# An order of work that knows of PSUM banks, and transposes that leave the score buffers

## The chip, the cores and the metric

The kernel runs on one core of a Trainium2 chip. The metric is the device time of one execution in microseconds. Before the change the median of three runs is 1225.1 us (1224.89 to 1226.91).

The core's engines work side by side, each through its own queue in order: TensorE (PE) multiplies matrices and transposes, and writes only to PSUM; VectorE (DVE), ScalarE (ACT) and GpSimd (POOL) work element by element; SyncE (SP) issues the transfers. PSUM has banks of 512 fp32 columns. The kernel's eight banks are: score buffers `s0` and `s1` (two banks each), `o` (two banks, the sums of the feed-forward block's output), `h` (one bank, its hidden layer, in halves `h0` and `h1`) and `pv` (one bank).

## The reference

Attention over 8 batches, 8 heads, 576 positions and head size 64, with a threshold below the row's maximum, and then a feed-forward block with a squared ReLU:

```
scores = scale * (q @ k.T)
thresh = max(scores, axis=-1) - tau
scores = where(scores >= thresh, scores, -1e9)
attn   = exp(scores - max) / (sum + 1e-9)
x      = (attn @ v), heads joined          # 4608 tokens x 512
h      = x @ w_in                          # 512 -> 2048
g      = s * relu(h)**2 + b
out    = g @ w_out                         # 2048 -> 512
```

All of it is fp32.

## The kernel before

**Visits and tiles.** A visit is a pair of heads and half of the queries of a batch: 64 visits, `Visit` objects numbered `n`. A tile is 128 queries against 576 keys. A visit of the first half has four tiles; one of the second half has a fifth, with the last 64 queries of both heads. For each tile PE writes scores into a score buffer (L373 for pairs of tiles, L362 for the fifth tile, L384 and L395 in later visits); DVE scales them and takes the minimum of the negated row (L416), ACT takes the exponential (L427), DVE applies the threshold and sums (L430), DVE takes the reciprocal (L433). From visit 4 on POOL scales the weights by it (L435); in visits 0 to 3 this is done after the values.

**Turning the weights.** The value product needs the weights with keys on the partitions. In visits 0 to 7 (`vs.pe`, `PE_VISITS = 8`) PE transposes them: four blocks of 128 columns into `tp` (L447) and the last 64 columns into `tt` (L445); ACT copies both into `er` (L456 and L454). Before the change `tt` is the first 128 columns of the tile's own score buffer, whose scores begin at column 224, so both share a bank. `tp` is `h` for even tiles of visits 0 to 3, and `pv` otherwise. From visit 8 on DVE transposes, and PE takes no part.

**Score buffers.** `scores_in` (L295) gives a tile its buffer: in visits 0 to 3 the three of `s0`, `s1` and `o` in turn; in visits 4 to 11 (`late`) `s0` and `s1` for the two tiles of a pair; later `s0` and `s1` in turn.

**Values and feed-forward block.** The value products of a visit (L498, L507) go through `pv`, from where ACT and DVE take x (L520 to L528). When four visits have given the x of 256 tokens, a block follows: 16 steps, each with a product into a half of `h` (L637), ReLU, square and rounding on ACT (L644 to L647), a remainder on POOL (L648) and two products into `o` (L654). The weights of the block are unpacked once, during the first block, by ACT, DVE and POOL (L582 to L596).

**The order of the work.** No engine's order is written by hand. Each step of each engine is put into a plan (`Plan.add`) with a cost, the keys that it reads and writes, and a due time. `Plan.ordered` builds an order forward or backward by list scheduling, `Plan.played` plays it with random delays, and `Plan.run` takes the best of 27 settings with 8 rounds each, by the mean over `SLOW` (a seed, and a factor on PE's costs early on). Keys are names such as `"s0"`; `(sk, "t")` is the key of the transposed 64 columns. In this plan they are no part of `"s0"`. When the kernel is built, accesses of two engines to one bank of a buffer are nevertheless put one after the other, in the order that the plan gave, by waits on semaphores.

Of the kernel before, what the change touches and what calls it, by code (L numbers as in the profile page):

```python
# [32 lines left out]
class Plan:  # L33
# [6 lines left out]
    SLOW = (1, 1.2), (2, 1.3), (3, 1.5), (4, 1.3)  # L40
# [6 lines left out]
    def add(self, engine, cost, emit, r=(), w=(), at=0.0, port=False, tiled=False):  # L47
# [12 lines left out]
        self.ops.append((engine, cost[0], cost[-1], emit, deps, at, port or engine == "POOL", tiled))  # L60
# [32 lines left out]
    def played(self, order, seed, cold, hand=60, to_pe=150, same=40):  # L93
        ops, free, done, port, mode = self.ops, {}, [0.0] * len(self.ops), 0.0, False
        late = random.Random(seed)
        for _, n in order:
            e, busy, ready, _, deps, _, shared, tiled = ops[n]
# [21 lines left out]
            done[n] = t + busy + tail  # L119
        return max(done) / 1000  # L120

    def ordered(self, before, after, rank, busy, done, back):
# [10 lines left out]
        order, port, mode = [], 0.0, False  # L133
        for _ in ops:
# [17 lines left out]
            if e == "PE" and mode and not ops[n][7]:  # L152
                for at, m in sorted(there[e]):
                    if ops[m][7] and at < rank[n] + self.NEAR:
# [8 lines left out]
            if ops[n][6] and port > t + self.PASS:  # L163
                for at, m in sorted(there[e]):
                    if not ops[m][6] and busy[m] < port - t + self.OVER:
                        there[e].remove((at, m))
                        heapq.heapify(there[e])
                        heapq.heappush(there[e], (rank[n], n))
                        n = m
                        break  # L170
            if ops[n][6]:
                t = max(t, port)
                port = t + busy[n]
            order.append((t, n))
# [17 lines left out]
def tile_attention_ffn(ctx: ExitStack, tc: tile.TileContext, qT, kT, v, tau, w_in, w_out, s, b, out):  # L192
# [91 lines left out]
    class Visit:  # L284
# [10 lines left out]
        def scores_in(self, i, j):  # L295
            return f"s{i % 2}" if self.split else f"s{j}" if self.late else ("s0", "s1", "o")[i % 3]
# [59 lines left out]
    def scores(vs, i, t):  # L356
        n = vs.n
        if t is None:
# [4 lines left out]
            pe(970, both, [("k", n)] + vs.kd, ["s0"], i - SCORES_AHEAD)  # L363
# [13 lines left out]
    def split_scores(vs, i, j, t):  # L377
# [8 lines left out]
        pe(531, products, [(x, j) for x in ("z", "qh", "ql")], [sk], i - SCORES_AHEAD)  # L386
# [22 lines left out]
    def tile_of(vs, i, j, t):  # L409
# [28 lines left out]
        if vs.pe:  # L438
            tt, kt = ps[0:T, 0:P], (sk, "t")
            kp = ["pv"] if vs.late or i % 2 else ["h0", "h1"]  # L440
            tp = bank[kp[0].strip("01")]
            tp = tp.rearrange("p (c q) -> p c q", c=NQ)

            def transposes():
                nc.tensor.transpose(out=tt, in_=ev[:, M:S], identity=ident)  # L445
# [4 lines left out]
            for h, n0, c0, c1 in parts:  # L450
                nn = (c1 - c0) // 32
                e = er[:, vs.n, h, n0:n0 + nn].rearrange("p n (c q) -> p c n q", c=5)
                ke = [("er", vs.n, h, n0 + n) for n in range(nn)]
                act((46 + 28 * nn, 146 + 28 * nn), lambda e=e, c0=c0, c1=c1, nn=nn: nc.scalar.copy(  # L454
                    out=e[0:T, NQ], in_=tt[:, c0:c1].rearrange("p (n q) -> p n q", n=nn)), [kt], ke, i + 0.5)
                act((68 + 100 * nn, 176 + 100 * nn), lambda e=e, c0=c0, c1=c1, nn=nn: nc.scalar.copy(  # L456
                    out=e[:, 0:NQ], in_=tp[:, :, c0:c1].rearrange("p c (n q) -> p c n q", n=nn)), kp + ke, ke, i + 0.5)
# [152 lines left out]
    class Block:  # L610
# [16 lines left out]
        def step(self, f, at):  # L627
# [10 lines left out]
            if f in (0, NF - 1):  # L638
                for c in range(0, NC, 2):
                    pe(6 * 120.9, lambda c=c: products(range(c, c + 2)), [("xh", c // 2), ("xl", c // 2), (f"w{f}", "i")], ["h0", "h1"], at)  # L640
            else:
                pe(3 * NC * 120.9, lambda: products(range(NC)), [(x, c) for x in ("xh", "xl") for c in range(2)] + [(f"w{f}", "i")],
# [222 lines left out]
```

## Time and profile before

| | |
|---|---|
| median of three runs | 1225.1 us |
| the profiled execution's own time | 1225.36 us |
| its span | 1223.5 us |
| PE busy | 1194.7 us (98%) |
| DVE busy | 802.5 us (66%) |
| ACT busy | 766.9 us (63%) |
| POOL busy | 700.8 us (57%) |
| chain that ended last, PE's share | 94% |

The span runs from the first to the last instruction of one profiled execution. Busy time is the time in which an engine has at least one instruction under way; a wait is idle time of an engine, put down to the instruction whose end released it. The chain that ended last goes back from the last instruction to what released it, step by step.

### The profile page before, as it was taken

How to read it: one execution, taken by the hardware profiler on the slowest of the kernel's cores; microseconds unless marked ns; L12 is line 12 of the kernel's file. 1: busy time of each engine (PE TensorE's matmuls, PEld its weight loads, DVE VectorE, ACT ScalarE, POOL GpSimd, SP SyncE). 2: the span in 40 equal slices, each digit the busy share in tenths (PEclk: the TensorE clock that was granted, in tenths of full speed). 3: DMA queues.
4: the chain of work that ended last, by engine and by line, in shares of the span. 5: the costliest groups of instructions: out<-in, count | busy, mean ns of one | idle time of the engine just before them, and what ended most of it. 6: DMA issues, size and time to landing. Idle time of an engine off the chain costs nothing.

```text
span 1223.5 us, 24575 instructions
## 1 busy us (share of the span) xinstructions
PE 1194.7 (98%) x7958; PEld 987.4 (81%) x7958; DVE 802.5 (66%) x2162; ACT 766.9 (63%) x1890; POOL 700.8 (57%) x806
## 2 busy tenths in 40 slices
PE   7789999999999999999999999999999999999998
PEld 5467778888887888878887888888888888878987
DVE  7997876777776776756666667666666576663021
ACT  5777756666665765666666666566656665654443
POOL 1466845766665775656675666667656675652200
PEclk8999999999999999999999999999999999999999
DMA  8661256677767766666566756556756666652000
GB/s 301 210 206 43 64 137 157 155 184 184 179 153 173 185 169 162 155 157 169 138 172 166 172 142 157 142 151 159 193 137 158 156 159 152 170 134 69 4 18 18
DMA packets 259536, 180.69 MB, mean 148 GB/s; under 512 B 83536, under 2 KB 238160, under 8 KB 259408
## 3 DMA queue, kind: packets, MB, share of 16 engines
q1 hardware_dynamic: 259120, 178.98, 57.5%
q8 instruction: 64, 1.05, 0.4%
q14 instruction: 64, 0.52, 0.1%
q10 hardware_dynamic: 288, 0.13, 0.0%
HBM read 87.03 MB, written 9.44 MB: 79 GB/s over the span
## 4 chain that ended last, share of the span: by engine, by line
PE 94%; DVE 3%; ACT 1%; issue 1%; DMA 0%; ACTq 0%; DVEq 0%
PE h L637 34%; PE o L654 33%; PE pv L507 13%; PE s L384 9%; PE s L373 2%; PE s L395 1%; DVE s L416 1%; DVE k L587 1%; PE pv L447 1%; DVE tr L430 0%; DMA qr<-in_q_dram 0%; DVE em L430 0%; PE s L445 0%; ACT em L427 0%; ACT er L456 0%
## 5 line engine op out<-in xcount | busy, mean ns | idle before, releaser
L637 PE MATMUL h<-xh,w 128*128 128x256 f32 x2304 | 467.0, 284 | 1.2 <-ACT g L644 1.2
L637 PEld LDWEIGHTS h<-xh,w 128*128 128x128 f32 x2304 | 377.5, 190 | 28.1 <-issue 7.6
L654 PE MATMUL o<-w,gh 128*128 128x512 f32 x1152 | 364.9, 398 | 0.6 <-DVE em L674 0.6
L416 DVE TENSOR_SCALAR_CACHE_REDUCE s<-s,nsc 128x576 f32<-128x576 f32 x283 | 230.4, 820 | 153.8 <-PE s L384 119.5
L648 POOL TENSOR_TENSOR gl<-g,gh 128x256 fp32r<-128x256 f32 x272 | 204.6, 753 | 212.7 <-ACT gh L647 187.1
L637 PE MATMUL h<-xl,w 128*128 128x256 f32 x1152 | 325.1, 282 | 0.0
L435 POOL TENSOR_SCALAR em<-em,st,zero 128x576 f32<-128x576 f32 x262 | 220.0, 841 | 139.2 <-DVE st L433 94.1
L430 DVE SCALAR_TENSOR_TENSOR em<-s,st,em 128x577 f32<-128x577 f32 x268 | 217.0, 811 | 83.9 <-ACT st L425 54.1
L427 ACT ACTIVATE em<-s,st 128x576 f32<-128x576 f32 x268 | 197.7, 738 | 66.9 <-DVE s L416 41.0
L654 PEld LDWEIGHTS o<-w,gh 128*128 128x128 f32 x1152 | 196.5, 189 | 35.1 <-issue 11.3
L654 PE MATMUL o<-w,gl 128*128 128x512 f32 x576 | 224.5, 390 | 0.0
L644 ACT ACTIVATE g<-h 128x256 f32<-128x256 f32 x288 | 110.4, 383 | 181.2 <-PE h L637 165.4
L637 PEld LDWEIGHTS h<-xl,w 128*128 128x128 f32 x1152 | 219.0, 190 | 5.5
L468 DVE STREAM_TRANSPOSE tr<-em 128x512 f32<-128x512 f32 x252 | 178.1, 707 | 52.0 <-POOL em L435 45.4
L507 PE MATMUL pv<-er,vb 128*64 128x256 f32 (+1 forms) x1280 | 170.3, 411 | 0.0
L349 POOL TENSOR_TENSOR k<-kr,k 64x576 fp32r<-64x576 f32 x104 | 149.0, 1434 | 37.1 <-ACT k L348 26.9
L647 ACT CAST gh<-g 128x256 fp32r<-128x256 f32 x288 | 116.2, 404 | 43.2 <-PE o L654 40.2
L384 PE MATMUL s<-k 128*128 128x288 f32 x832 | 142.4, 296 | 0.0
L507 PEld LDWEIGHTS pv<-er,vb 128*64 128x64 f32 x1280 | 85.7, 136 | 66.8 <-issue 11.8
L384 PEld LDWEIGHTS s<-k 128*128 128x128 f32 x832 | 127.2, 188 | 15.3 <-issue 2.4
L654 PEld LDWEIGHTS o<-w,gl 128*128 128x128 f32 x576 | 108.2, 188 | 24.6
L645 ACT ACTIVATE g<-g 128x256 f32<-128x256 f32 x288 | 120.0, 417 | 4.8
(108 smaller groups left out, 939.5 us busy)
## 6 DMA issues: line engine op xcount, KB each, us to landing
er<-tr SPq DMA_DIRECT2D x448, 160.0 KB, 3.2
kr<-in_k_dram SPq DMA_DIRECT2D x116, 288.0 KB, 4.1
vb<-in_v_dram SPq DMA_DIRECT2D x128, 128.0 KB, 3.0
qr<-in_q_dram SPq DMA_DIRECT2D x56, 160.0 KB, 4.3
er<-tr SPq DMA_DIRECT2D x112, 80.0 KB, 2.3
w<-in_moe_w_in_dram SPq DMA_DIRECT2D x16, 512.0 KB, 6.3
w<-in_moe_w_out_dram SPq DMA_DIRECT2D x16, 512.0 KB, 5.4
out_dram<-oo SPq DMA_DIRECT2D x30, 256.0 KB, 2.3
```

The costliest lines, as they stand in the source:

```text
L349: pool((1500, 1500), lambda: nc.gpsimd.tensor_tensor(out=z()[D:P], in0=kr[D:P, j], in1=z()[D:P].bitcast(F32), op=ALU.subtract), rk + [("z" ...
L384: nc.tensor.matmul(flat[sk][:, S0 + hf * HS:S0 + (hf + 1) * HS], lazy["q"][:, x, j, qc], lazy["k"][:, j, cs], start=(x == 0), stop=(x == 1))
L416: dve((740, 875), lambda: nc.vector.tensor_scalar(out=ps[:, S0:S0 + S], in0=ps[:, S0:S0 + S], scalar1=nsc, scalar2=None, op0=ALU.mult, op1 ...
L427: act((632, 740), lambda: nc.scalar.activation(out=ev, in_=ps[:, S0:S0 + S], func=AF.Exp, bias=st8[:, 0:1], scale=-1.0), [sk, (ks_, 0)], [ ...
L430: dve((742, 830), lambda: nc.vector.scalar_tensor_tensor(out=eb, in0=ps[:, S0:S0 + S + 1], scalar=st8[:, 1:2], in1=eb, op0=ALU.is_le, op1= ...
L435: pool((795, 825), lambda: nc.gpsimd.tensor_scalar(out=ev, in0=ev, scalar1=st8[:, 4:5], scalar2=zero, op0=ALU.mult, op1=ALU.add), [em_k, ( ...
L468: nc.vector.transpose(out=to[:, :, 0:NQ].rearrange("p m c q -> p m (c q)"), in_=ev[:, 0:M].rearrange("p (m r) -> p m r", m=4))
L507: nc.tensor.matmul(ps[j * D:(j + 1) * D, 0:32 * nb], vb[r, n, j, c], er[r, n, j, 0:nb, 32 * c:32 * c + 32], start=(c == 0), stop=(c == 4))
L637: nc.tensor.matmul(ps, w[:, c, :], x[:, c, :], start=(c == 0 and i == 0), stop=(c == NC - 1 and i == 2))
L645: act((322, 417), lambda: nc.scalar.activation(out=g, in_=g, func=AF.Square), [f"g{k}"], [f"g{k}"], at)
L648: do((712, 740), lambda: eng.tensor_tensor(out=lo, in0=g, in1=hi.bitcast(F32), op=ALU.subtract), [f"g{k}", f"gh{n}"], [f"gl{n}"], at)
L654: nc.tensor.matmul(bank["o"][:, t, :], a[:, ts_], w, start=(f == 0 and i == 0), stop=(f == NF - 1 and i == 2))
```

## The change

It has three parts.

1. The plan notes for each step which PSUM banks it touches and whether it writes there (`banks`, `use`). `free_at` lets a step start only when the last accesses of other engines to the bank are over, where one of the two writes; `used` notes the access. `played` and `ordered` both apply it. If a step would have to wait for a bank or for the port that DVE and POOL share by more than `PASS`, another ready step of the engine may go first.
2. In visits 0 to 3 scores use `s0` and `s1` alone. The transposes become two steps: even tiles use `h` for the 512 columns and `o[:, 1]` for the 64, odd tiles `o[:, 0]` and `pv`. In visits 4 to 7 both go through `pv`: 512 columns, their copies, then the 64 columns into the same bank, and their copies.
3. Constants of the plan change: the factors of `SLOW`, and some costs of PE's steps. The second products name `o0` or `o1` in place of `o`. A guard column for scores in `o` is no longer set.

```diff
-    SLOW = (1, 1.2), (2, 1.3), (3, 1.5), (4, 1.3)
+    SLOW = (1, 1.0), (2, 1.1), (3, 1.3), (4, 1.1)
...
+        use = {b: False for k in r for b in self.banks(k)}
+        use.update((b, True) for k in (*w, *(r if engine == "PE" else ())) for b in self.banks(k))
+        self.ops.append((engine, cost[0], cost[-1], emit, deps, at, port or engine == "POOL", tiled, tuple(use.items())))
+
+    def banks(self, k):
+        k, t = k if isinstance(k, tuple) and len(k) == 2 else (k, None)
+        if k == "o":
+            return [f"o{t}"] if t in (0, 1) else ["o0", "o1"]
+        return [k] if k in ("s0", "s1", "pv", "o0", "o1") else ["h"] if k in ("h0", "h1") else []
+
+    def free_at(self, n, t, last, tail, hand):
+        for b, writes in self.ops[n][8]:
+            for e, wrote, at, rest in last.get(b, ()):
+                if e != self.ops[n][0] and (writes or wrote):
+                    t = max(t, at + (rest if tail is None else tail) + hand)
+        return t
+
+    def used(self, n, at, rest, last):
+        for b, writes in self.ops[n][8]:
+            was = last.get(b, []) if not writes else []
+            last[b] = [u for u in was if u[1] or u[0] != self.ops[n][0]] + [(self.ops[n][0], writes, at, rest)]
...
+            if ops[n][8]:
+                t = self.free_at(n, t, last, None, to_pe if e == "PE" else hand)
...
+        def delay(n, t):
+            at = max(t, port) if ops[n][6] else t
+            if not ops[n][8]:
+                return at - t
+            hand = self.TO_PE if ops[n][0] == "PE" else self.HANDOVER
+            return self.free_at(n, at, last, done[n] - busy[n] if back else None, hand) - t
...
+            wait = delay(n, t)
+            if wait > self.PASS:
+                for at, m in sorted(there[e]):
+                    if delay(m, t) <= self.PASS and busy[m] < wait + self.OVER:
+                        there[e].remove((at, m))
+                        heapq.heapify(there[e])
+                        heapq.heappush(there[e], (rank[n], n))
+                        n, wait = m, delay(m, t)
+                        break
+            t += wait
...
-            return f"s{i % 2}" if self.split else f"s{j}" if self.late else ("s0", "s1", "o")[i % 3]
+            return f"s{i % 2}" if self.split else f"s{j}"
...
-            pe(970, both, [("k", n)] + vs.kd, ["s0"], i - SCORES_AHEAD)
+            pe(760, both, [("k", n)] + vs.kd, ["s0"], i - SCORES_AHEAD)
...
-            tt, kt = ps[0:T, 0:P], (sk, "t")
-            kp = ["pv"] if vs.late or i % 2 else ["h0", "h1"]
-            tp = bank[kp[0].strip("01")]
+            if vs.late:
+                tp, kp = bank["pv"], ["pv"]
+                tt, kt = tp[0:T, 0:P], kp
+            elif i % 2:
+                tt, kt, tp, kp = bank["pv"][0:T, 0:P], ["pv"], bank["o"][:, 0], ["o0"]
+            else:
+                tt, kt, tp, kp = bank["o"][0:T, 1, 0:P], ["o1"], bank["h"], ["h0", "h1"]
...
-            pe(575, transposes, [em_k, "ident"], [kt] + kp, i + 0.5)
...
+            pe(390, whole, [em_k, "ident"], kp, i + 0.5)
+            if kt != kp:
+                pe(90, rest, [em_k, "ident"], kt, i + 0.5)
+            copies(True)
+            if kt == kp:
+                pe(90, rest, [em_k, "ident"], kt, i + 0.5)
+            copies(False)
...
-                pe(3 * 231.3, lambda t=t: second(t), [f"gh{n}", f"gl{n}", (f"w{f}", "o")],
-                   [("o", t)] + (["o"] if f == 0 else []), at + SECOND)
+                pe(3 * 230.4, lambda t=t: second(t), [f"gh{n}", f"gl{n}", (f"w{f}", "o")],
+                   [("o", t)] + ([f"o{t}"] if f == 0 else []), at + SECOND)
```

`whole` holds the four transposes of 128 columns, `rest` the one of 64; `copies(True)` makes the copies of the first, `copies(False)` those of the second.

## Rows read from the trace of the kernel before

**Rows 1.** The page: busy time of an engine, busy tenths and clock in 40 slices.
```profile
PE 1194.7 (98%) x7958; PEld 987.4 (81%) x7958; DVE 802.5 (66%) x2162; ACT 766.9 (63%) x1890; POOL 700.8 (57%) x806
...
PE   7789999999999999999999999999999999999998
...
PEclk8999999999999999999999999999999999999999
```

**Rows 2.** Busy time by stage: stretch, its length, busy us of each engine, clock.
```profile
9.00:80.00 71.00, 53.52 (x338) 34.97 (x338) 67.54 (x187) 53.22 (x112) 27.19 (x22) 0.89 0.78 262
80.00:112.00 32.00, 32.00 (x212) 23.95 (x209) 27.12 (x70) 25.69 (x65) 25.72 (x23) 1.00 0.27 84
112.00:122.00 10.00, 7.96 (x53) 5.97 (x51) 6.69 (x18) 6.11 (x16) 3.56 (x5) 1.00 0.01 2
...
200.00:1100.00 900.00, 900.00 (x6096) 753.79 (x6095) 619.98 (x1687) 579.39 (x1446) 576.37 (x663) 1.00 0.66 161
1100.00:1223.50 123.50, 117.64 (x738) 102.72 (x736) 21.78 (x49) 50.67 (x127) 19.13 (x26) 1.00 0.10 27
```

**Rows 3.** Waits of PE and of DVE, 9 to 80 us: total, times, longest.
```profile
PE s L373 <- DVE tr L430: 2.9, 2, 2.4
PE pv L447 <- ACT er L456: 2.4, 3, 1.2
PE pv L447 <- DVE x L521: 1.9, 2, 1.6
PE s L445 <- ACT tr L427: 1.8, 2, 1.5
...
PE s L373 <- ACT er L454: 1.4, 1, 1.4
...
DVE s L416 <- PE s L373: 3.0, 2, 2.7
...
DVE s L416 <- PE s L445: 0.9, 1, 0.9
DVE s L416 <- ACT er L454: 0.7, 2, 0.4
```

**Rows 4.** PE's instructions in order of time, 53 to 78 us: start, length, instruction, idle before.
```profile
53.16 1.24 PE L373 MATMUL s<-kr,qr 64*128 64x288 f32 x8 [0.50 <-DVE tr L430]
...
60.66 1.97 PE L373 MATMUL s<-kr,qr 64*128 64x288 f32 x8
...
68.13 0.66 PE L447 MATMUL pv<-k,em 128*128 128x128 f32 x4 [0.38 <-DVE x L521]
...
70.43 0.66 PE L447 MATMUL pv<-k,em 128*128 128x128 f32 x4 [1.21 <-ACT er L456]
70.84 0.36 PE L637 MATMUL h<-xh,w 128*128 128x256 f32 x1
...
77.26 0.27 PE L445 MATMUL s<-k,tr 128*64 128x128 f32 x1 [1.49 <-ACT tr L427]
```

**Rows 5.** ACT's instructions in order of time, 69 to 116 us.
```profile
69.64 0.26 ACT L454 COPY er<-s 64x128 f32<-64x128 f32 x1 [0.91 <-DVE s L416]
...
76.37 0.74 ACT L427 ACTIVATE tr<-s,st 128x576 f32<-128x576 f32 x1
...
114.72 0.26 ACT L454 COPY er<-s 64x128 f32<-64x128 f32 x1 [3.16 <-PE s L373]
114.88 0.58 ACT L456 COPY er<-pv 128x512 f32<-128x512 f32 x1
```

**Rows 6.** PE's instructions in order of time, 115 to 121 us.
```profile
115.51 0.66 PE L447 MATMUL pv<-k,em 128*128 128x128 f32 x4 [0.59 <-ACT er L456]
...
117.04 0.38 PE L637 MATMUL h<-xh,w 128*128 128x256 f32 x1 [0.17 <-ACT g L644]
...
120.01 0.27 PE L445 MATMUL s<-k,tr 128*64 128x128 f32 x1 [1.27 <-DVE tr L430]
```

**Rows 7.** DVE's instructions in order of time, 115 us.
```profile
115.01 0.83 DVE L416 TENSOR_SCALAR_CACHE_REDUCE s<-s,nsc 128x576 f32<-128x576 f32 x1 [2.13 <-ACT er L454]
```

**Rows 8.** DVE's L587: its group from 9 to 80 us; its durations, whole span.
```profile
L587 DVE SCALAR_TENSOR_TENSOR k<-w,k 128x512 int32<-128x512 int32 x14 | 12.0, 857 | 0.0
...
L587 DVE SCALAR_TENSOR_TENSOR k<-w,k x28: 669/685/1635, 21.8 to 142.9; 128x512 int32<-128x512 int32 x28
```

More of the change, by code (lines that the diff above doesn't have):

```diff
@@ L94, in played @@
         ops, free, done, port, mode = self.ops, {}, [0.0] * len(self.ops), 0.0, False
-        late = random.Random(seed)
+        late, last = random.Random(seed), {}
         for _, n in order:
-            e, busy, ready, _, deps, _, shared, tiled = ops[n]
+            e, busy, ready, _, deps, _, shared, tiled, _ = ops[n]
             t = free.get(e, 0.0)
@@ L119, in played @@
             done[n] = t + busy + tail
+            if ops[n][8]:
+                self.used(n, t + busy, tail, last)
         return max(done) / 1000
@@ L132, in ordered @@
                 heapq.heappush(coming[o[0]], (0.0, n))
-        order, port, mode = [], 0.0, False
+        order, port, mode, last = [], 0.0, False, {}
+        def delay(n, t):
[4 more added lines that the diff above has]
+            return self.free_at(n, at, last, done[n] - busy[n] if back else None, hand) - t
         for _ in ops:
@@ L162, in ordered @@
                 mode = ops[n][7]
[L163 to L170, printed above, removed]
             if ops[n][6]:
-                t = max(t, port)
                 port = t + busy[n]
+            if ops[n][8]:
+                self.used(n, t + busy[n], done[n] - busy[n], last)
             order.append((t, n))
@@ L385, in products @@
                                      start=(x == 0), stop=(x == 1))
-        pe(531, products, [(x, j) for x in ("z", "qh", "ql")], [sk], i - SCORES_AHEAD)
+        pe(526, products, [(x, j) for x in ("z", "qh", "ql")], [sk], i - SCORES_AHEAD)
     def last_rows(vs, i, before):
@@ L442, in tile_of, with whole, rest @@
             tp = tp.rearrange("p (c q) -> p c q", c=NQ)
-            def transposes():
-                nc.tensor.transpose(out=tt, in_=ev[:, M:S], identity=ident)
+            def whole():
                 for c in range(NQ):
                     nc.tensor.transpose(out=tp[:, c], in_=ev[:, c * P:(c + 1) * P], identity=ident)
-            pe(575, transposes, [em_k, "ident"], [kt] + kp, i + 0.5)
+            def rest():
+                nc.tensor.transpose(out=tt, in_=ev[:, M:S], identity=ident)
@@ L449, in tile_of, with copies @@
             parts = [(j, 4 * t, 0, P)] if t is not None else [(h, NB // 32, h * T, h * T + T) for h in range(2)]
[L450 to L457, printed above, removed]
+            def copies(first):
+                for h, n0, c0, c1 in parts:
+                    nn = (c1 - c0) // 32
+                    e = er[:, vs.n, h, n0:n0 + nn].rearrange("p n (c q) -> p c n q", c=5)
+                    ke = [("er", vs.n, h, n0 + n) for n in range(nn)]
+                    if first:
+                        act((68 + 100 * nn, 176 + 100 * nn), lambda e=e, c0=c0, c1=c1, nn=nn: nc.scalar.copy(
+                            out=e[:, 0:NQ], in_=tp[:, :, c0:c1].rearrange("p c (n q) -> p c n q", n=nn)), kp, ke, i + 0.5)
+                    else:
+                        act((46 + 28 * nn, 146 + 28 * nn), lambda e=e, c0=c0, c1=c1, nn=nn: nc.scalar.copy(
+                            out=e[0:T, NQ], in_=tt[:, c0:c1].rearrange("p (n q) -> p n q", n=nn)), kt + ke, ke, i + 0.5)
@@ L639, in step @@
                 for c in range(0, NC, 2):
-                    pe(6 * 120.9, lambda c=c: products(range(c, c + 2)), [("xh", c // 2), ("xl", c // 2), (f"w{f}", "i")], ["h0", "h1"], at)
+                    pe(6 * 120, lambda c=c: products(range(c, c + 2)), [("xh", c // 2), ("xl", c // 2), (f"w{f}", "i")], ["h0", "h1"], at)
             else:
-                pe(3 * NC * 120.9, lambda: products(range(NC)), [(x, c) for x in ("xh", "xl") for c in range(2)] + [(f"w{f}", "i")],
+                pe(3 * NC * 120, lambda: products(range(NC)), [(x, c) for x in ("xh", "xl") for c in range(2)] + [(f"w{f}", "i")],
                    ["h0", "h1"], at)
@@ L726, in guards @@
     def guards():
-        for n in "s0", "s1", "o":
+        for n in "s0", "s1":
             nc.vector.memset(flat[n][:, S0 + S:S0 + S + 1], -3e38)
```

3 lines of the change are left out of this document (1 added, 2 removed).

## Prediction

> **What bounds the kernel now.** I read the page first, then busy time by stage, then who waits for whom in the stages where TensorE is not full, and last the few microseconds around each such wait. On the page TensorE (PE) is busy 98% of the span, and the slices below nine tenths are the first three and the last; its granted clock is below nine tenths in the first slice alone [rows 1]. The stages say the same in microseconds [rows 2]: from 200 to 1100 us PE is busy 900.00 of 900.00 us at clock 1.00, so no order of the work can gain anything there except by giving PE less to do, and the change takes no matmul away. What is left is 9 to 80 us, where PE idles 71.00 - 53.52 = 17.5 us, the stretch from 112 to 122 us, where it idles 10.00 - 7.96 = 2.0 us, and the end (123.50 - 117.64 = 5.9 us), which holds no transposes and which the change leaves alone. Between 9 and 80 us the engine to look at is VectorE (DVE): busy 67.54 of 71.00 us, 95%. PE's matmuls for the feed-forward block begin at 70.84 us [rows 4]; until then PE lives on what DVE hands it. So a gain has to come from idle DVE before about 70 us or from idle PE behind it, some 20 us altogether, and most of those are waits for real data.
>
> **What the trace shows of the banks.** In the kernel before, the last 64 columns of a tile are transposed into the first 128 columns of a score buffer (L445) and copied out by ScalarE (ACT) at L454. Those columns share a bank with the scores. In visits 4 to 7 a tile's weights are scaled by POOL (L435) before PE may transpose them, so a wait of L445 on ACT's exponential (L427) can't be one for its data: it is the exponential of another tile that is reading the same bank. The trace has such waits in every direction: PE's L445 for L427, 1.8 us; PE's scores for the copy L454, 1.4 us; DVE's L416 for L445 and for L454, 0.9 and 0.7 us [rows 3]. From 112 to 122 us they form one chain: L454 starts at 114.72 after ACT idled 3.16 us behind scores that PE writes in that bank [rows 5], DVE's L416 starts at 115.01 after 2.13 us behind L454 [rows 7], and PE, which has run out of other work, waits 0.59 us for pv, 0.17 us for g and 1.27 us for the threshold (L430) [rows 6].
>
> **The change part by part.**
> *The 64 columns leave the score buffers (all eight visits).* Terms that go:
> - the hole from 112 to 122 us, 0.59 + 0.17 + 1.27 = 2.0 us [rows 6]. PE is the bound around it, so it counts in full.
> - the wait of 1.49 us of L445 at 77.26 us for an exponential that starts at 76.37 us [rows 4, 5]. Feed-forward matmuls stand behind it in PE's queue; counted in full, 1.5 us.
> - the wait of 1.21 us of pv at 70.43 us [rows 4]: ACT's L454 before it had idled 0.91 us for DVE's L416 in the same bank [rows 5]; 0.9 us.
> - DVE's waits for L445 and L454 from 9 to 80 us, 0.9 + 0.7 = 1.6 us [rows 3]. DVE is the bound there, so PE's waits of the same stretch don't count again; but a DVE that is early helps PE only where PE then has work, so I take the middle between 0 and 1.6, 0.8 us. The ends are 0 and, with PE's 1.4 us, 3.0 us.
> Sum: 2.0 + 1.5 + 0.9 + 0.8 = 5.2 us.
>
> *In visits 4 to 7 both transposes go through pv, one after the other.* PE transposes 512 columns, ACT copies (0.58 us), and only then PE transposes the other 64 (0.27 us) and ACT copies again (0.26 us); a handover is 0.05 us (the copy that starts at 114.88 ends at 115.46, PE starts at 115.51) [rows 5, 6]. pv is held 0.27 + 0.05 + 0.26 + 0.05 = 0.63 us longer per tile, for 20 tiles. Behind the second transpose wait, in PE's queue, whatever the plan put there, and everything else that needs pv: the next tile's transposes and the value products. After 80 us feed-forward matmuls can stand between (PE is busy 32.00 of 32.00 us from 80 to 112 us [rows 2]) and the cost is nothing; if that cover failed, each tile would pay 0.63 us. Ahead of 80 us there is hardly any cover. Bounds: 0 and 20 x 0.63 = 12.6 us. I take the places in these visits where PE already waits for pv before 80 us: at 68.13 us (0.38 us, for x to be read out by L521) and at 70.43 us [rows 4]; 2 x 0.63 = 1.3 us.
>
> The row just used shows PE waiting 1.21 us for a bank that ACT is still emptying. The Trainium skill ("Perfetto Trace Analysis", section "Matmuls") says that independent matmul groups should rotate through different PSUM banks, so that emptying one overlaps filling the next. By that rule the second pass through pv costs at every tile, 12.6 us by the upper bound, not at two; the trace agrees before 80 us, and after it shows the wait covered.
>
> *Visits 0 to 3 use two score buffers in place of three; "o" and "h" or pv and "o" take the transposes.* The scores of a pair of tiles can then be written only when both tiles before are through L430. PE needs 1.24 us for a pair at full clock and 1.97 us at the lower one [rows 4], and DVE has no tile work meanwhile. Its other work (unpacking weights) fills such gaps: L587 alone is 12.0 us from 9 to 80 us [rows 8]. Bounds: 0, and 7 pairs x 1.97 = 13.8 us. I take 0: visits 4 to 7 already run on two buffers, and DVE's busy share of 95% covers part of them as well [rows 2].
>
> *The plan's model and constants.* It moves every instruction, the DMAs on SP among them; no wait that PE or DVE has from 9 to 80 us is for SP or POOL among the larger ones [rows 3]. What it can still win is DVE's stretching: L587 takes 857 ns in the mean of 14 against a median of 685 ns, 14 x 0.172 = 2.4 us [rows 8], while POOL works beside it. Ends: 2.4 us won, and as much lost; I take 0. One memset fewer and five transposes per tile as before: 0.
>
> Sum: 5.2 - 1.3 = 3.9 us off. The profiled execution took 1225.36 us (1.86 us outside its span), so 1221.5 us. The median of the runs, 1225.1 us, lies 0.3 us lower; the forecast is 3.6 us or 0.29% below it. A difference under 0.2% (2.45 us) is what I call no change.
>
> **The rivals.**
> *pv takes the place of the score buffers.* Four tiles of visits 4 to 7 pass through pv before 80 us (the last at the row of 77.26 us), and about as many where PE runs out of other work as it does from 112 to 122 us. If seven pay 0.63 us in place of two, 3.2 us more go: 1221.5 + 3.2 = 1224.7 us, no change. For it: PE's waits on pv are already 2.4 and 1.9 us from 9 to 80 us [rows 3]. Against it: a plan that knows the bank can put value products or scores between the two passes. The rule of the Trainium skill ("Perfetto Trace Analysis", section "Matmuls") leads here too.
> *Two score buffers starve DVE.* In visits 0 to 3 the gap of a pair that no weight work covers costs between 1.24 and 1.97 us, 1.6 in the middle. Five uncovered gaps of seven cost 8.0 us: 1221.5 + 8.0 = 1229.5 us, slower. It decides from four gaps on (3.6 us of gain plus 2.45 us, over 1.6 us). For it: DVE waits 3.0 us for scores already, PE 2.9 us for DVE to be through with a buffer [rows 3]. Against it: 2.7 us of those 3.0 are the first wait, before any scores exist, and there is more weight work than gaps.
> *The feed-forward work starts earlier too.* Nothing is lost at pv and DVE's stretching goes: 5.2 + 2.4 = 7.6 us, 1217.8 us. For it: the plan now sees every wait that it schedules around. Against it: the stretching is no matter of banks.
> *The change doesn't do what it says:* the new order keeps as many waits, in other places, 1225 us.
>
> **How the numbers follow.** Forecast 0.38, pv 0.27, starved DVE 0.17, earlier start 0.13, no effect 0.05. About a fifth of the forecast's case lies within 0.2% of the median, and a little of pv's lies on either side: faster 0.30 + 0.13 + 0.02 = 0.45, the same 0.08 + 0.21 + 0.04 = 0.33, slower 0.17 + 0.04 + 0.01 = 0.22. The range reaches from 1215.5 us (the earlier start with the 3.0 us of the upper end in place of 0.8) to 1228.5 us (short of five starved gaps). The forecast's own range is 1218.5 to 1223.5 us.
>
> **What would show it.** Right: no wait of L416 for the copy of the 64 columns and none of the transposes for L427; from 112 to 122 us (or where visits 4 to 7 end) PE full; PE's idle time from 9 to 80 us smaller by 2 to 4 us; the page's PE busy time the same within 2 us. pv as rival: waits of the transposes for the copies (L456 before) over 5 us in total. Starved DVE: waits of L416 for scores (L373) beyond 3.0 us, and DVE under 93% busy from 9 to 80 us. I am wrong in kind if the idle time after 200 us changes, since no step above reaches there.

## The result, and the profile after

The changed kernel takes 1232.92 us (median of 5 runs, 1232.47 to 1234.28) against 1225.87 us for the kernel before, measured beside it: a ratio of 1.0054, 95% interval 1.0043 to 1.0066. I forecast 1221.5 us. The change made the kernel slower, and the time lies outside the range.

The page of the kernel after, the lines that answer to [rows 1], with its chain that ended last:

```profile
PE 1193.8 (97%) x7958; PEld 985.8 (80%) x7958; DVE 802.6 (65%) x2161; ACT 766.8 (62%) x1890; POOL 702.0 (57%) x806
...
PE   6789999999999999999999999999999999999998
...
PEclk7899999999999999999999999999999999999999
...
PE 92%; DVE 4%; DMA 2%; ACT 1%; issue 1%; SPq 0%; POOL 0%; DVEq 0%; ACTq 0%
```

PE has as many instructions as before, x7958, and is busy 0.9 us less, in a span that is 7.2 us longer (1230.7 against 1223.5 us). So all of the loss is PE standing idle, 8.1 us more of it. The stages of the kernel after (stretch, length, busy us of PE, PEld, DVE, ACT and POOL, clock) say where; after them stand three of the kernel before, for stretches that [rows 2] does not have as rows of their own:

```profile
9.00:80.00 71.00, 50.29 (x323) 32.38 (x324) 66.58 (x181) 51.69 (x106) 29.24 (x22) 0.86 0.77 258
112.00:122.00 10.00, 9.31 (x57) 7.10 (x56) 8.57 (x19) 7.78 (x18) 6.66 (x6) 1.00 0.06 22
122.00:150.00 28.00, 26.65 (x175) 19.93 (x175) 21.05 (x50) 21.67 (x59) 20.21 (x23) 1.00 0.13 34
...
80.00:200.00 120.00, 115.65 (x753) 87.69 (x752) 93.55 (x238) 84.84 (x208) 73.25 (x81) 1.00 0.37 97
200.00:1100.00 900.00, 896.97 (x6061) 752.05 (x6060) 614.12 (x1673) 574.79 (x1439) 574.58 (x659) 1.00 0.66 160
1100.00:1230.70 130.70, 125.91 (x803) 109.44 (x801) 26.92 (x63) 54.15 (x138) 22.94 (x31) 1.00 0.13 34
```

```profile
0.00:9.00 9.00, 5.53 (x26) 4.77 (x26) 1.13 (x9) 1.28 (x1) 1.98 (x15) 0.92 0.71 219
...
122.00:150.00 28.00, 28.00 (x188) 20.94 (x188) 23.07 (x52) 21.68 (x57) 22.16 (x25) 1.00 0.18 47
...
80.00:200.00 120.00, 117.96 (x769) 91.11 (x766) 92.11 (x232) 82.38 (x208) 76.13 (x82) 1.00 0.37 96
```

PE's idle time grows from 17.5 to 20.7 us between 9 and 80 us [rows 2], from 2.0 to 4.4 us between 80 and 200 us, and from nothing to 3.0 us between 200 and 1100 us; before 9 us it grows by 0.6 us (9.00 - 4.96 against 9.00 - 5.53), and after 1100 us it shrinks by 1.1 us. The hole from 112 to 122 us shrinks, as forecast, to 0.7 us idle in place of 2.0 us. But the 1.3 us are not won: from 122 to 150 us, where PE had no idle time before, it now idles 1.4 us, and all 2.0 us of idle time from 112 to 150 us are waits for copies out of pv. The waits (who waited for whom: total us, times, longest) name what came instead, for PE over the whole span and, in the last line, for DVE from 9 to 80 us:

```profile
PE h L484 <- DVE tr L464: 6.7, 3, 3.8
PE pv L548 <- ACT er L499: 6.3, 3, 2.7
PE h L484 <- DVE em L464: 5.0, 2, 2.8
PE pv L487 <- ACT er L496: 2.7, 4, 0.9
...
PE pv L484 <- ACT er L499: 1.5, 3, 0.6
PE o L704 <- DVE oo L724: 1.4, 3, 0.8
...
PE pv L557 <- ACT er L499: 0.5, 1, 0.5
...
DVE s L450 <- PE s L407: 5.7, 6, 2.3
```

And of the kernel before, PE's waits that answer to the first three lines:

```profile
PE o L445 <- DVE tr L430: 1.6, 1, 1.6
PE s L445 <- DVE tr L430: 1.4, 2, 1.3
...
PE pv L498 <- ACT er L456: 1.3, 1, 1.3
```

In the kernel after, L407 writes scores, L450 scales them, L464 is the threshold, L484 and L487 are the transposes of the 512 and of the 64 columns, L496 and L499 their copies, L548 the first value product. No transpose waits for another tile's exponential any more, and L450 waits for no copy: every wait inside the score buffers that [rows 3], [rows 6] and [rows 7] show is gone. In their place PE waits 11.7 us for thresholds before it can transpose (6.7 + 5.0, against 1.6 + 1.4 before) and 6.3 us for the copies before a value product (against 1.3), and DVE waits 5.7 us for scores against 3.0 us.

PE's instructions in order of time show the pattern (start, length, instruction, idle before):

```profile
42.07 0.27 PE L487 MATMUL pv<-k,em 128*64 128x128 f32 x1
46.11 1.12 PE L484 MATMUL h<-k,tr 128*128 128x128 f32 x4 [3.77 <-DVE tr L464]
...
47.37 2.10 PE L407 MATMUL s<-kr,qr 64*128 64x288 f32 x8
...
52.38 0.99 PE L484 MATMUL h<-k,em 128*128 128x128 f32 x4 [2.22 <-DVE em L464]
...
64.65 0.66 PE L548 MATMUL pv<-k,st 128*64 128x128 f32 x8 [2.73 <-ACT er L499]
...
70.24 0.30 PE L487 MATMUL pv<-k,em 128*64 128x128 f32 x1 [0.86 <-ACT er L496]
71.11 0.63 PE L484 MATMUL pv<-k,em 128*128 128x128 f32 x4 [0.58 <-ACT er L499]
...
72.60 0.49 PE L687 MATMUL h<-xh,w 128*128 128x256 f32 x1
```

With two score buffers a pair of tiles goes through as one, and PE and DVE run in lockstep: PE writes both, DVE and ACT work on both, and PE has nothing to write meanwhile, because both buffers are taken (3.77 and 2.22 us). Then PE runs and DVE waits for scores. The feed-forward matmuls begin at 72.60 us, 1.8 us later than in [rows 4].

### The profile page after: what moved, and what is told of

Read it like the earlier page. It is cut to its first block, busy times and chain, and to the rows that moved or that the text cites. A ratio compares the mean times of both kernels' runs of the same rounds, so it can differ in the third digit from the quotient of the medians.

```text
span 1230.7 us, 24541 instructions
## 1 busy us (share of the span) xinstructions
PE 1193.8 (97%) x7958; PEld 985.8 (80%) x7958; DVE 802.6 (65%) x2161; ACT 766.8 (62%) x1890; POOL 702.0 (57%) x806
## 4 chain that ended last, share of the span: by engine, by line
PE 92%; DVE 4%; DMA 2%; ACT 1%; issue 1%; SPq 0%; POOL 0%; DVEq 0%; ACTq 0%
PE h L687 33%; PE o L704 32%; PE pv L557 13%; PE s L418 9%; PE s L407 2%; PE s L429 1%; DVE s L450 1%; DMA qr<-in_q_dram 1%; PE pv L484 1%; DVE em L464 0%; ACT em L461 0%; DVE tr L464 0%; DVE xl L673 0%; DVE k L637 0%; DMA vb<-in_v_dram 0%
## 5 line engine op out<-in xcount | busy, mean ns | idle before, releaser
L450 DVE TENSOR_SCALAR_CACHE_REDUCE s<-s,nsc 128x576 f32<-128x576 f32 x288 | 234.1, 821 | 157.8 <-PE s L418 119.9
L464 DVE SCALAR_TENSOR_TENSOR em<-s,st,em 128x577 f32<-128x577 f32 x270 | 218.5, 812 | 98.3 <-ACT st L459 58.9
L557 PE MATMUL pv<-er,vb 128*64 128x256 f32 (+1 forms) x1280 | 171.9, 414 | 1.5 <-DMA out_dram<-oo 1.0
L557 PEld LDWEIGHTS pv<-er,vb 128*64 128x64 f32 x1280 | 86.5, 137 | 67.9 <-issue 11.6
```

The source lines that it names most:

```text
L450: dve((740, 875), lambda: nc.vector.tensor_scalar(out=ps[:, S0:S0 + S], in0=ps[:, S0:S0 + S], scalar1=nsc, scalar2=None, op0=ALU.mult, op1 ...
L464: dve((742, 830), lambda: nc.vector.scalar_tensor_tensor(out=eb, in0=ps[:, S0:S0 + S + 1], scalar=st8[:, 1:2], in1=eb, op0=ALU.is_le, op1= ...
L557: nc.tensor.matmul(ps[j * D:(j + 1) * D, 0:32 * nb], vb[r, n, j, c], er[r, n, j, 0:nb, 32 * c:32 * c + 32], start=(c == 0), stop=(c == 4))
```

## The experiments

I held three theories. **Theory 1:** the new buffers cost by themselves (1a two score buffers, 1b the banks that take the 64 columns early, 1c two passes through pv in visits 4 to 7). **Theory 2:** the plan's new model or constants choose a worse order. **Theory 3:** any new order differs from the next by several us by chance, and the order before was a good draw. All times are medians beside runs of the kernel before on the same chip (its medians were 1226.0 to 1227.2 us), so I compare the ratios. Each edit is shown against the kernel that it starts from, before or after; `...` marks what is left out.

### Round one: which part of the change

**layout_only**, the new buffers under the plan before:

```diff
 class Plan:                      # all of it, SLOW and the costs as before
-            return f"s{i % 2}" if self.split else f"s{j}" if self.late else ("s0", "s1", "o")[i % 3]
+            return f"s{i % 2}" if self.split else f"s{j}"
...                               # transposes, copies and the key of o as after the change
```

> Before's plan, its SLOW and its costs, with the changed kernel's buffers: two score buffers in visits 0 to 3, the 64 columns out of the score buffers, through pv in visits 4 to 7. Theory 1 (the buffers cost: PE and DVE run in lockstep on two score buffers in visits 0 to 3, and the value products wait for the 64 columns in pv): 1229 to 1233 us, and from 9 to 80 us PE idles 20 us or more, with waits of the transposes for the threshold over 8 us. Theory 2 (the plan's new model or constants choose a worse order, the buffers gain the 3 to 4 us that I forecast): 1221 to 1225 us. Theory 3 (any new order differs by chance by several us): anywhere from 1221 to 1233 us.

Measured: 1238.07 us, ratio 1.0089 (1.0073 to 1.0104). Above even theory 1's range. Its stages, and PE's waits from 9 to 80 us (here L450 is the transpose, L514 the value product, L465 the copy):

```profile
9.00:80.00 71.00, 49.18 (x284) 30.55 (x281) 62.10 (x166) 47.38 (x95) 25.15 (x20) 0.82 0.71 237
```

```profile
PE h L450 <- DVE tr L430: 8.9, 4, 3.4
PE pv L514 <- ACT er L465: 5.7, 4, 1.9
PE h L450 <- DVE em L430: 2.8, 1, 2.8
```

PE idles 71.00 - 49.18 = 21.8 us there, 11.7 us of it for thresholds, the same pattern as in the changed kernel; DVE drops to 62.10 us, 87%.

**model_only**, the reverse: the new model, everything else as before.

```diff
+        use = {b: False for k in r for b in self.banks(k)}
...                               # banks, free_at, used, delay added; buffers, SLOW and costs of before
```

> Before's buffers, costs and SLOW, with the plan's new model of banks and of what may pass. Theory 1: not slower, 1221 to 1226 us, since the waits inside the score buffers are now seen and planned around. Theory 2: 1229 to 1233 us. Theory 3: anywhere from 1221 to 1233 us.

Measured: 1228.67 us, ratio 1.0017 (1.0009 to 1.0026). Between theories 1 and 2: the model alone does cost something, 2 us and not 3 or more.

**const_only**, the kernel before with the new SLOW and PE costs.

```diff
-    SLOW = (1, 1.2), (2, 1.3), (3, 1.5), (4, 1.3)
+    SLOW = (1, 1.0), (2, 1.1), (3, 1.3), (4, 1.1)
...
-            pe(970, both, [("k", n)] + vs.kd, ["s0"], i - SCORES_AHEAD)
+            pe(760, both, [("k", n)] + vs.kd, ["s0"], i - SCORES_AHEAD)
```

> The kernel before with only the changed SLOW and PE costs. Theory 1: 1224 to 1227 us. Theory 2, if it is the constants: 1229 to 1233 us. Theory 3: anywhere from 1221 to 1233 us.

Measured: 1228.89 us, ratio 1.0017 (1.0009 to 1.0026). Between the ranges of theories 1 and 2, and again 2 us for nothing but another order.

**after_oldconst**, the changed kernel with the SLOW and the costs of before.

```diff
-    SLOW = (1, 1.0), (2, 1.1), (3, 1.3), (4, 1.1)
+    SLOW = (1, 1.2), (2, 1.3), (3, 1.5), (4, 1.3)
...                               # and the five costs of PE's steps
```

> The changed kernel with before's SLOW and PE costs (buffers and model new). Theory 1: 1230 to 1234 us, as the changed kernel. Theory 2, if it is the constants: 1221 to 1226 us; if it is the model: 1230 to 1234 us. Theory 3: anywhere from 1221 to 1233 us.

Measured: 1233.88 us, ratio 1.0060 (1.0047 to 1.0074). On the new buffers the constants are not the cause. Against model_only, which differs in the buffers and their keys alone, it is 0.43% slower.

### Round two: which buffers

**late_only** and **early_only** take back one half of the change of buffers each. late_only names all of `o` again as well, as the kernel before does; early_only doesn't.

```diff
 late_only
-            return f"s{i % 2}" if self.split else f"s{j}"
+            return f"s{i % 2}" if self.split else f"s{j}" if self.late else ("s0", "s1", "o")[i % 3]
...
+                tt, kt = ps[0:T, 0:P], [(sk, "t")]
+                kp = ["pv"] if i % 2 else ["h0", "h1"]      # visits 0 to 3
 early_only
-                tt, kt = tp[0:T, 0:P], kp
+                tt, kt = ps[0:T, 0:P], [(sk, "t")]          # visits 4 to 7
```

> The changed kernel with visits 0 to 3 as before: three score buffers, the 64 columns in the score buffer, h or pv for the rest. Visits 4 to 7 stay changed (both transposes through pv), as do model and constants. If the early buffers cost (theory 1): 1223 to 1228 us. If the two passes through pv in visits 4 to 7 cost (theory 1c): 1229 to 1233 us.

> The changed kernel with visits 4 to 7 as before: the 64 columns in the score buffer, the rest in pv. Visits 0 to 3 stay changed. Theory 1: 1230 to 1235 us. Theory 1c: 1224 to 1229 us.

Measured: late_only 1232.27 us, ratio 1.0048 (1.0035 to 1.0061); early_only 1229.39 us, ratio 1.0019 (1.0010 to 1.0028). late_only lies in the range of theory 1c, early_only 0.4 us above it and below that of theory 1: that speaks for 1c, against what I had come to think.

**two_ts** keeps two score buffers in visits 0 to 3 but puts the 64 columns back into them (o stays unused); **three_tp** gives visits 0 to 3 three score buffers and sends the 64 columns through the bank of the rest, as in visits 4 to 7, with all of `o` named again.

```diff
 two_ts
-                tt, kt, tp, kp = bank["pv"][0:T, 0:P], ["pv"], bank["o"][:, 0], ["o0"]
-                tt, kt, tp, kp = bank["o"][0:T, 1, 0:P], ["o1"], bank["h"], ["h0", "h1"]
+                tt, kt = ps[0:T, 0:P], [(sk, "t")]
+                kp = ["pv"] if i % 2 else ["h0", "h1"]
 three_tp
-            return f"s{i % 2}" if self.split else f"s{j}"
+            return f"s{i % 2}" if self.split else f"s{j}" if self.late else ("s0", "s1", "o")[i % 3]
...
+            kp = ["pv"] if vs.late or i % 2 else ["h0", "h1"]
+            tp = bank[kp[0].strip("01")]
+            tt, kt = tp[0:T, 0:P], kp
```

> The changed kernel, in visits 0 to 3 two score buffers, but the 64 columns in the score buffer and the rest in h or pv, as before; o is left unused there. If two score buffers in place of three cost (theory 1a): 1229 to 1236 us, waits of DVE's L450 for scores (or of PE for thresholds) as in the changed kernel. If it is the 64 columns in pv and o, where the value products wait for their copies (theory 1b): 1224 to 1228 us.

> The changed kernel, in visits 0 to 3 three score buffers again, and the 64 columns after the rest through the same bank (h for even tiles, pv for odd ones). So no transposes in score buffers anywhere, but a third buffer. Theory 1a: 1220 to 1227 us, below the kernel before if the waits inside the score buffers were worth what I forecast. Theory 1b, and the rival that a second pass through a bank costs wherever there is no cover: 1229 to 1234 us, with waits of the second transposes for the copies over 8 us from 9 to 80 us.

Measured: two_ts 1235.83 us, ratio 1.0073 (1.0060 to 1.0085), as theory 1a says, with 9.6 us of waits for thresholds ahead of the transposes into h. three_tp 1230.77 us, ratio 1.0034 (1.0022 to 1.0047), inside the range of theory 1b and its rival and not below the kernel before; but their mark is not there: its second transposes wait 4.6 us for copies from 9 to 80 us, not over 8 us. Its first stages:

```profile
9.00:20.00 11.00, 8.77 (x29) 5.01 (x26) 8.67 (x28) 6.35 (x13) 0.00 (x0) 1.00 1.03 378
20.00:30.00 10.00, 9.27 (x57) 5.59 (x54) 10.00 (x28) 8.40 (x18) 2.73 (x3) 1.00 0.64 219
30.00:40.00 10.00, 7.79 (x27) 5.03 (x29) 8.96 (x24) 6.40 (x14) 5.16 (x4) 0.54 0.36 115
...
80.00:90.00 10.00, 10.00 (x53) 5.96 (x52) 6.38 (x19) 4.27 (x12) 2.59 (x4) 0.73 0.31 102
```

The third buffer does what it should: PE idles 14.0 us from 9 to 80 us, against 20.7 us in the changed kernel. But PE is busy 1204.4 us with the same 7958 matmuls, 10.6 us more than in the changed kernel, and so most of the idle time that went came back as busy time. PE's granted clock falls to 0.54 in one stretch and to 0.73 in another, but the clock doesn't settle it: from 9 to 80 us it is 0.89 here and 0.86 in the changed kernel. Why the same matmuls keep PE busy longer is not shown.

### Round three: how much is chance

**before_seed1**, **before_seed2** and **after_seed1** change the seeds of SLOW.

```diff
-    SLOW = (1, 1.2), (2, 1.3), (3, 1.5), (4, 1.3)
+    SLOW = (5, 1.2), (6, 1.3), (7, 1.5), (8, 1.3)
```

> The kernel before, with the seeds of SLOW 5 to 8 in place of 1 to 4 and nothing else changed: its plan only picks another of its candidate orders, or the same. Theory 3 (an order differs from the next by chance, and the order of the kernel before is a good draw): 1227 to 1231 us. Theory 1 (the time follows from the buffers): 1225 to 1227 us.

> As the last, with the seeds 9 to 12. Theory 3: 1227 to 1231 us, not the same as with the seeds 5 to 8. Theory 1: 1225 to 1227 us.

> The changed kernel with the seeds 5 to 8. Theory 1: 1231 to 1235 us. Theory 3: 1227 to 1235 us, several us from the changed kernel; a value below 1228 us would say that the buffers cost nothing.

Measured: ratios 1.0003 (0.9994 to 1.0011), 0.9998 (0.9989 to 1.0006) and 1.0074 (1.0058 to 1.0090). These say nothing on the theories: the seeds select the same order, instruction for instruction, on every engine (in the trace of before_seed2 twelve of PE's 7958 matmuls, products of two score tiles that run side by side, start in another sequence). The plan tries 18 settings, not the 27 that are named ahead; a seed only chooses among their orders, where LATER makes others. The three are repeats, and show that an order gives its time again: spans of 1223.5, 1223.5 and 1223.8 us before, 1230.7 and 1230.1 us after; the ratio of the changed kernel is 0.2% apart in its two measurements.

**after_okey** makes the plan treat `o` as one in the feed-forward block, as before.

```diff
-                   [("o", t)] + ([f"o{t}"] if f == 0 else []), at + SECOND)
+                   [("o", t)] + ([f"o{t}", "o"] if f == 0 else []), at + SECOND)
...
-                    dve((664 // parts + 40, 750 // parts + 50), take, [("o", t), "bias", "s_"],
+                    dve((664 // parts + 40, 750 // parts + 50), take, ["o", ("o", t), "bias", "s_"],
```

> The changed kernel, but the second products and the read-out of a block name all of o again, so that the plan takes the next block's first products to wait for both halves. In the changed kernel PE idles 3.0 us from 200 to 1100 us, 1.4 us of it for the read-out of o. If the key is behind this: under 1 us of idle there, 1229 to 1231 us. If it is only how the order fell: no shift that can be told, 1231 to 1235 us, idle of 1 to 4 us there.

Measured: 1237.94 us, ratio 1.0099 (1.0086 to 1.0112), above both ranges. From 200 to 1100 us PE idles 0.9 us and no longer 3.0 us, as the expectation for the key said, but the order of the first 80 us came out worse (clock 0.76 there, against 0.86), and the whole is 5 us slower. A change of one key far from the start re-drew the start.

**before_p1**, **after_p1**, **early_only_p1** and **late_only_p1** are four of the kernels with another amount of spare time in the plan.

```diff
-    LATER = 1.0, 1.2, 1.4
+    LATER = 1.1, 1.3, 1.5
```

> The kernel before with LATER = 1.1, 1.3, 1.5 in the plan (how much spare time a step is given), which gives every engine another order and touches nothing else: one more draw of an order for the buffers of before. Theory 3 (chance of the order is most of the 7 us): 1229 to 1235 us. Theory 1 (the buffers are most of it, chance is some 2 us): 1225 to 1229 us.

> The changed kernel with the same LATER: one more draw of an order for its buffers. Theory 3: anywhere from 1225 to 1238 us. Theory 1: 1231 to 1238 us.

> early_only (new buffers in visits 0 to 3, old ones in visits 4 to 7) with the same LATER. If the new buffers of visits 0 to 3 cost nothing, as its first order (1229.4 us) says beside the 1229 us of re-planned old buffers: 1226 to 1231 us. If they cost some 5 us and the first order was lucky: 1232 to 1238 us.

> late_only (old buffers in visits 0 to 3, pv twice in visits 4 to 7) with the same LATER. If the two passes through pv cost some 3 us, as its first order (1232.3 us) says: 1230 to 1235 us. If chance: 1225 to 1230 us.

Measured: before_p1 1232.85 us, ratio 1.0047 (1.0035 to 1.0059); after_p1 1239.89 us, 1.0113 (1.0100 to 1.0126); early_only_p1 1231.34 us, 1.0039 (1.0027 to 1.0051); late_only_p1 1231.81 us, 1.0047 (1.0033 to 1.0061). The kernel before loses 0.47% by a new order alone, nearly as much as the change cost: theory 3 holds for that. Yet after_p1 goes past the ranges of both theories. early_only_p1 lies 0.3 us above the range in which the early buffers cost nothing, late_only_p1 in the range in which two passes through pv cost.

**model_const** and **model_const_p1** close the pairs: model and constants of after on the buffers of before, with both values of LATER.

```diff
 class Plan:                      # as after the change
-            return f"s{i % 2}" if self.split else f"s{j}"
+            return f"s{i % 2}" if self.split else f"s{j}" if self.late else ("s0", "s1", "o")[i % 3]
...                               # transposes, copies and keys of before
```

> The changed kernel's model and constants on the buffers of before: against the changed kernel only the buffers differ. The two pairs measured so far (layout_only against the kernel before, after_oldconst against model_only) differ by 11 and 5 us. If the buffers cost under any plan: 1224 to 1230 us, 3 us or more below the changed kernel. If chance is all: as likely above as below the changed kernel's 1233 us, 1226 to 1239 us.

> As model_const, with LATER = 1.1, 1.3, 1.5; its partner is after_p1 (1239.9 us). If the buffers cost under any plan: 1227 to 1236 us. If chance is all: as likely above as below 1239.9 us.

Measured: model_const 1230.34 us, ratio 1.0036 (1.0024 to 1.0047), 0.3 us above the range of theory 1, and less than 3 us below the changed kernel; model_const_p1 1227.25 us, ratio 1.0009 (1.0000 to 1.0017), inside the range of theory 1. The stretch from 9 to 80 us and PE's waits in it, first of model_const_p1, then of its partner after_p1, which differs from it in the buffers and their keys alone:

```profile
9.00:80.00 71.00, 59.18 (x345) 38.20 (x343) 67.27 (x188) 53.57 (x112) 26.64 (x22) 0.95 0.74 250
...
PE s L407 <- ACT er L488: 2.9, 3, 1.7
PE s L407 <- DVE em L464: 1.8, 1, 1.8
```

```profile
9.00:80.00 71.00, 49.81 (x284) 31.57 (x284) 63.49 (x164) 47.44 (x95) 25.25 (x19) 0.77 0.69 232
...
PE pv L548 <- ACT er L499: 6.2, 4, 1.9
PE h L484 <- DVE tr L464: 5.2, 4, 2.1
...
PE h L484 <- DVE em L464: 2.8, 1, 2.8
```

With the old buffers PE idles 71.00 - 59.18 = 11.8 us and runs at clock 0.95; with the new ones it idles 21.2 us, 8.0 us of it for thresholds and 6.2 us for copies before value products, and runs at 0.77.

### What the runs say together

Four pairs of kernels differ in the buffers alone, with the keys that go with them, that of `o` among them (ratios to the kernel before; PE's idle time from 9 to 80 us, its length less PE's busy time):

| plan | old buffers | new buffers | difference | PE idle, old | PE idle, new |
|---|---|---|---|---|---|
| before | 1 | 1.0089 (layout_only) | +0.89% | 17.5 us | 21.8 us |
| new model | 1.0017 (model_only) | 1.0060 (after_oldconst) | +0.43% | 18.0 us | 19.8 us |
| new model and constants | 1.0036 (model_const) | 1.0054 (the change) | +0.18% | 14.1 us | 20.7 us |
| the same, other LATER | 1.0009 (model_const_p1) | 1.0113 (after_p1) | +1.04% | 11.8 us | 21.2 us |

The new buffers are slower in all four, by 0.6% in the mean, and PE idles more in all four. That bears theory 1 out, though not pair by pair: under the plan of the change itself the buffers are worth the least, 0.18%, which is no more than the distance between the two measurements of the changed kernel. Of its 0.54%, 0.36% (0.24 to 0.47) come with the new model and constants on the old buffers; what goes with the buffers is 0.18%, or 0.38% by the repeat (after_seed1). And theory 3 holds beside it: the other five plans that I ran on the old buffers have ratios of 1.0017, 1.0017, 1.0047, 1.0036 and 1.0009. The order of the kernel before is the best of six, and these re-plannings lose 0.25% in the mean (3 us).

The two losses are of different kinds. Over the whole span (its length less PE's busy time) the new buffers add about 7, 4, 10 and 12 us of idle time in the four pairs, while PE's busy time moves by about +7, +1, -7 and -1 us. The five re-planned orders on the old buffers lose in busy time: PE is busy 2.8 to 7.3 us longer than before with the same 7958 matmuls, and its idle time changes by between -4.6 and +2.6 us. Two of them, model_const (span 1228.2 us) and model_const_p1 (1226.2 us):

```profile
PE 1201.1 (98%) x7958; PEld 990.5 (81%) x7958; DVE 798.4 (65%) x2162; ACT 766.4 (62%) x1890; POOL 703.8 (57%) x806
```

```profile
PE 1202.0 (98%) x7958; PEld 991.1 (81%) x7958; DVE 800.2 (65%) x2162; ACT 765.3 (62%) x1890; POOL 696.6 (57%) x806
```

One comparison prices the forecast's main term by itself. three_tp and model_const have the same model, constants, number of score buffers and keys of `o`; in three_tp the 64 columns have left the score buffers in all eight visits, by a second pass through h or pv. The ratios are 1.0034 and 1.0036, and PE idles 14.0 and 14.1 us from 9 to 80 us. So taking those waits away gained nothing that can be told, in this one plan.

Which half of the buffers costs isn't settled by the times. Going from two score buffers to three gains 0.25% with the 64 columns in them (two_ts to late_only) and 0.20% without (the change to three_tp). Going to two passes through pv in visits 4 to 7 costs 0.12% and 0.38% (late_only against model_const, late_only_p1 against model_const_p1), and 0.35% and 0.74% where the early half is new (the change against early_only, after_p1 against early_only_p1). The early half by itself gives -0.17% and +0.30% (early_only, early_only_p1, against model_const and model_const_p1), and +0.06% and +0.66% where the late half is new. Most of these are no larger than the spread of the five orders on the old buffers, 0.09% to 0.47%. PE's idle time from 9 to 80 us speaks more evenly: with two score buffers it is 1.8 to 6.7 us longer than with three in all six comparisons that change the early half alone under one plan. The late half goes with 3.3 to 4.4 us more in its four, but three_tp, which has it too, idles no more than model_const. No kernel that I ran beats the kernel before.

## Why the prediction was wrong

**What bounds the kernel** was right: PE, and before about 80 us DVE with it. **The waits inside the score buffers** were read rightly and did go. What failed is the step from a wait to a gain. The sum took 5.2 us off as if PE would then be busy. From 80 to 200 us, where 2.0 us of it lay, PE idled 2.3 us more and not 2.0 us less. With the third score buffer kept (three_tp against model_const), the 64 columns' way out of the score buffers, 5.2 - 1.3 = 3.9 us off in the sum, measured some 0.2 us, which is within the noise.

**The step that failed first: "Visits 0 to 3 use two score buffers in place of three ... I take 0: visits 4 to 7 already run on two buffers, and DVE's busy share of 95% covers part of them as well."** DVE's share did hold: 66.58 of 71.00 us, 94%. But the argument looked at DVE alone. What a third buffer gave was work for PE while DVE had both others; without it PE waits for thresholds, 11.7 us, and for the last copies of a visit, 6.3 us. In visits 4 to 7 no such wait for a threshold is left with the same two buffers: feed-forward matmuls stand between there, and in visits 0 to 3 there are none. The waits for thresholds ahead of the transposes into h and for copies ahead of the value product, 14 us and more together, stand in the change, layout_only and after_p1. They are not lost in their full length: early_only has 16.3 us of them (9.7 + 2.8 + 3.8) and is no slower than model_const, which has other waits. What is left is the 1.8 to 6.7 us more of idle time from 9 to 80 us, where the sum had 0. My bound of 13.8 us was wide enough; the value in it was wrong. The rival "Two score buffers starve DVE" had the right place and sign, 1229.5 us, and named the wrong victim: of its two marks, the waits of L450 for scores rose (5.7 us against 3.0), while DVE stayed above 93%.

The Trainium skill ("Perfetto Trace Analysis", section "Optimization Strategy") says that the same gap, repeating on the engine that should be saturated, can mean that there are too few buffers for the next tile. These traces agree: five gaps of up to 3.77 us ahead of L484, and 14.0 us of idle time in place of 20.7 us when the third buffer is given back.

**The second: "The plan's model and constants ... Ends: 2.4 us won, and as much lost; I take 0."** It measured +0.36%, 4.4 us of 1226 us, nearly twice the end. I had bounded it by one thing that I could see (the stretching of L587), where the plan moves every instruction. What it cost lies in a term that the sum did not have: in model_const PE is busy 1201.1 us against 1194.7 us, 6.4 us more for the same matmuls, and idles 1.7 us less. What lengthens the busy time stays open. The trace of one order can't show how good a draw it is; the five others lie 0.09% to 0.47% above it.

**pv in visits 4 to 7** was sized at 1.3 us. In these visits PE waits 2.7 + 1.5 + 0.5 = 4.7 us for copies out of pv (the lines with L487, L484 and L557 above). Before, its waits on pv there were 1.21 and 0.38 us [rows 4] and 0.59 us [rows 6], 2.2 us together: 2.5 us more. The mechanism was right, the size was a little over half. 2.0 us of the 4.7 us lie after 80 us, where the sum put the cost at nothing, although [rows 6] has PE waiting 0.59 us for pv there. The mark that I had set for pv as rival, over 5 us of waits of the transposes for the copies, was not reached (2.7 + 1.5 = 4.2 us).

**After 200 us** no step of mine reached, and I wrote that idle time there would prove me wrong in kind. It did: 3.0 us, 1.4 us of it for the read-out of o, whose two halves the plan now treats apart. With one key again (after_okey) it is 0.9 us. The other three pairs agree in sign: 1.2 us against 0.0, 0.8 against 0.3 and 5.0 against 0.6 us, new buffers and keys first.

**The range** reached to 1228.5 us and left out even the 1229.5 us of a rival that I had given a chance of 0.17. It should have reached past 1232 us: the starved gaps, the lost draw and pv can all come at once, and I had added them one at a time.

## What to carry to other kernels

When a plan of the whole order is re-run, the first thing to price is the draw itself: run a few orders that differ in a meaningless constant, and take a change for a gain or a loss only against that spread. A wait that a trace shows is worth its length only if its engine then has something to do; ask what else that engine could run, and which buffer lets it. Taking a buffer from a pipeline is judged at the engine that fills it, not only at the one that empties it.

## What the runs showed of the hardware

PE's granted clock fell behind long stalls of PE, though not behind each, and the work there took longer for it. After 15 us the changed kernel has five stalls over 2 us, ahead of 17.65 us (2.13 us), 24.35 us (2.42 us), 46.11 us (3.77 us), 52.38 us (2.22 us) and 64.65 us (2.73 us). The value products of visit 0, behind the second, take 4.11 us; those of visit 1, behind 1.14 us, and of visit 3, behind the fifth, take 2.48 us (PE's instructions in order of time, then stretches with the clock as the third number from the end):

```profile
24.35 0.66 PE L548 MATMUL pv<-k,st 128*64 128x128 f32 x8 [2.42 <-ACT er L499]
24.84 4.11 PE L557 MATMUL pv<-er,vb 128*64 128x256 f32 x20
...
37.46 2.48 PE L557 MATMUL pv<-er,vb 128*64 128x256 f32 x20
...
65.14 2.48 PE L557 MATMUL pv<-er,vb 128*64 128x256 f32 x20
```

```profile
18.40:21.80 3.40, 3.40 (x14) 2.21 (x13) 3.26 (x9) 1.91 (x5) 0.81 (x1) 0.50 1.04 357
24.84:28.90 4.06, 4.06 (x26) 1.80 (x22) 4.06 (x7) 1.59 (x3) 4.00 (x3) 0.58 0.04 12
37.46:39.90 2.44, 2.44 (x26) 1.24 (x22) 2.44 (x9) 2.10 (x4) 1.01 (x1) 1.00 1.07 344
46.11:49.10 2.99, 2.99 (x13) 2.05 (x13) 2.99 (x7) 2.26 (x5) 0.30 (x1) 0.50 0.85 285
52.60:55.70 3.10, 3.10 (x13) 1.71 (x11) 2.26 (x9) 2.40 (x6) 1.11 (x1) 0.50 0.02 5
65.14:67.50 2.36, 2.36 (x24) 1.20 (x20) 2.36 (x5) 1.18 (x2) 2.30 (x2) 1.00 0.94 354
```

A clock of 0.50 is the lower of the two levels, 1.2 GHz, and 0.58 is mostly that level; 1.00 is 2.4 GHz throughout. So behind four of the five stalls PE worked at the lower level, and behind the fifth it did not. The clock does not decide between the orders: from 9 to 80 us it runs from 0.76 (after_okey, 1237.9 us) to 0.95 (model_const_p1, 1227.3 us), but PE is busy 1202.0 us in model_const_p1 at 0.95 and 1193.8 us, the least of all, in the changed kernel at 0.86.
